# Attention and two MLPs in one kernel: the first part's weight sums move into the last slots of layer 1, the last output group is summed bank by bank, and the unused general path's transfers change queue

## The chip, the cores and the metric

One core of one Trainium2 chip runs the whole program. The metric is the device time of one execution in microseconds. TensorE is called PE here as in the profile, VectorE DVE, ScalarE ACT, GpSimd POOL and SyncE SP.

## The reference, cut to what matters

Attention with sinks and a window gives 1536 tokens of width 512. Two MLPs with 2048 inner columns follow; the second is the one that the change touches.

```
def _moe_ref(x, w_in, w_out, a, b):            # layer 1
    h = x @ w_in
    P = a[0] + a[1] * h + a[2] * h**2 + a[3] * h**3
    Q = 1.0 + abs(b[0]) * abs(h) + abs(b[1]) * h**2
    return (P / (Q + 1e-06)) @ w_out

def _moe2_ref(x, w_in, w_out):                 # layer 2
    h = np.maximum(x @ w_in, 0.0)
    return (h * h @ w_out)
```

The weights arrive as 64-bit floats and are converted on the chip. Every product is made of three matmuls on a high and a low part of each factor (high times high, high times low, low times high).

## The kernel before

**Slots of layer 1.** After the attention, the program is an order written out by hand. A step of layer 1 is one of 3 chunks of 512 tokens and one of 16 blocks of 128 inner columns, so there are 48 steps. In each slot PE gets twelve matmuls that make `h` of one step (`g1`, in `whole`, L635) and twelve that multiply the finished activation of an earlier step with the second weight (`g2`, L702). ACT, DVE and POOL work out the rational function between the two. The last of it is `act_c`: ACT writes the high part `gh` (L681) and POOL subtracts it from `g`, which gives the low part `gl` (L682). `gh` and `gl` have two buffers each. POOL also multiplies in L652, subtracts the high part of a converted weight in L282 (`w_fin`) and the high part of layer 1's output in L750 (`split_late`).

**Turns of layer 2.** Layer 2 works on four parts of four blocks each. The chunk of tokens 0 is multiplied in the plain way (`whole`). For chunks 1 and 2 a Winograd scheme takes seven products in place of eight for each of two pairs of blocks. It needs sums of the first weights (`weights_sums`: L794 and L801 on POOL, then a split into high and low, L805 on ACT and L806 on POOL) and sums of the tokens (`tokens_sums`: L815 on DVE, split by `tokens_split` through the same L805 and L806). `turn(n)` orders this by tables: `hs` says which products stand in a turn, `gs` in which turn which activation meets the second weight through `g2`, `ms` and `ss` where weight sums are made and split. The sums of the first part stand in turns 1 and 2 and their splits in turns 2 and 7. Turn 3 is the first with a `g2` of layer 2. Below, block 0 to block 3 are the four blocks of part 0 in chunk 0, whose `g2` stand in turns 3 to 6.

**Weights.** `jobs` is the list of loads and conversions. The first `LATE = 32 + AHEAD` weight tiles are converted during layer 1, the others in the turns that `CONV` names. All weights are also loaded a second time for a check of their size (L229 on DVE).

**The end.** The last four `g2`, those of part 3 and chunk 2, come one block after another, each over four PSUM banks. Then DVE adds each bank to the earlier partial sum (L736, in `finish`) and SP issues a transfer of 256 KB for each (L739). `verdict` reduces the checks to one flag, which all engines load (L1252). If it is not zero, `general()` computes everything again in a slower way; on these inputs it is zero, and each engine branches over that code (L1254) to the wait for all transfers and the end.

Of the kernel before, what the change touches and what calls it, by code (L numbers as in the profile page):

```python
# [15 lines left out]
P = 128  # L16
# [15 lines left out]
AHEAD = 10  # L32
# [3 lines left out]
CONV = (1, 9, 10, 12, 13, 15, 16, 17, 18, 19, 20, 22, 23, 27, 28, 29, 30, 31, 32, 34, 35, 36)  # L36
# [8 lines left out]
def kernel(  # L45
# [594 lines left out]
    def layers(mp, due):  # L640
# [44 lines left out]
        def g2(k):  # L685
            L, g, c, f = steps[k] if k in range(KL) else (1,) + k
            f0, f1 = part(L, g)[0], part(L, g)[1] - 1
            if f == f0:
                if f1 == NF - 1 and (L, c) == (1, NCH - 1):
                    acc[L, g, c] = [ps_t("T"), ps_t("T"), ps_t("U"), ps_s()[:, 0]]  # L690
                else:
                    acc[L, g, c] = [t[:, m] for t in [ps_s(), ps_s()] for m in range(2)]
# [89 lines left out]
        def setup_two():  # L782
            two["sum"], = tags(1)
            two["s"] = [tags(2), tags(2)]
            two["g"] = [t[:, j].bitcast(F32) for t in map(fresh, tags(4)) for j in range(2)]

        def weights_sums(p, r):
# [3 lines left out]
            y = z.rearrange("p a (b n) -> p (a b) n", b=2)  # L791
            for e in range(2):
                w = W[1, f + e, 0]
                nc.gpsimd.tensor_tensor(out=x[:, e], in0=w[0].bitcast(F32), in1=w[1].bitcast(F32), op=ALU.add)  # L794
            hw = DM // 2
            a11, a12, a21, a22 = (x[:, e, j * hw:(j + 1) * hw] for e in range(2) for j in range(2))
            for dst, i0, i1, op in (
                (y[:, 0], a21, a22, ALU.add), (y[:, 1], y[:, 0], a11, ALU.subtract),
                (y[:, 2], a11, a21, ALU.subtract), (y[:, 3], a12, y[:, 1], ALU.subtract),
            ):  # L800
                nc.gpsimd.tensor_tensor(out=dst, in0=i0, in1=i1, op=op)  # L801
            two["S", r] = lambda: split(z, fresh(tag[0]), fresh(tag[1]))
# [87 lines left out]

        def turn(n):
# [12 lines left out]
            if n == 3:  # L904
                tokens_sums()
            if n in hs:
# [7 lines left out]
            if n + 1 in gs:  # L914
                key = gs[n + 1]
                g = gq.pop(("f", key))
                act_c(key, g)
                two["g"].append(g)
            if n in ss:
                r = "S", ss[n]  # L920
                two[r] = two[r]()
            for j in ((2,), (3,), (1,), (4, 0))[n - 3] if 3 <= n < 7 else ():
                tokens_split(j)
            if n in ms:
                weights_sums(*ms[n])
# [3 lines left out]
        def slot(k, mid=None, after=None):  # L929
# [16 lines left out]
            split_late()  # L946
            w_until(due(k))
            if 0 <= k - 2 < K:
                g2(k - 2)
            if k + 1 - K in gs:  # L950
                g2(gs[k + 1 - K])
            if after:
                after()
            if k + 1 - K == ends2:
                finish(0)
                finish(1)

        return slot, K + ends2


# [40 lines left out]
    def general():  # L1001
        with ExitStack() as gx:
# [16 lines left out]
            with tc.tile_pool(name="ga", bufs=1) as ga:  # L1019
# [7 lines left out]
                for b in range(B):  # L1027
                    nc.sync.dma_start(out=kt, in_=k[b].rearrange("(r e) d t -> (e d) r t", e=2))
                    for i in range(NB):
                        nc.sync.dma_start(  # L1030
                            out=vt[:, i], in_=v[b, :, i * P:(i + 1) * P, :].rearrange("h p d -> p h d")
                        )
                    for i in range(NB):
                        nc.sync.dma_start(
# [66 lines left out]
            with tc.tile_pool(name="gm", bufs=1) as gm:  # L1101
                for L in range(2):
                    wg = [gm.tile([P, NF, DM], F32, name=f"wg{j}") for j in range(2)]
                    for f in range(NF):
                        for j in range(2):
                            src = ((w_in1, w_out1), (w_in2, w_out2))[L][j].bitcast(I32)
                            r = gs.tile([P, DM, 2], I32, tag="gr", name="gr")
                            if j == 0:
                                nc.sync.dma_start(
# [3 lines left out]
                            else:  # L1113
                                nc.sync.dma_start(
# [24 lines left out]
                    for c in range(NCH):  # L1139
# [59 lines left out]
                        for m in range(4):  # L1199
# [3 lines left out]
                            else:  # L1203
# [3 lines left out]
                                nc.sync.dma_start(out=out[r0:r0 + P, :], in_=o)  # L1207
# [20 lines left out]
    slot, slots = layers(mp, due)  # L1228
# [25 lines left out]
    with tc.If(flag != 0):  # L1254
# [40 lines left out]
```

## Time and profile before

| what | value |
|---|---|
| median of 3 runs | 604.63 us (604.2 to 605.49) |
| the profiled execution, its own time | 605.5 us |
| its span | 603.7 us |
| granted clock of PE, mean | 0.994 |
| busy in the span | PE 588.8, DVE 441.3, POOL 414.6, ACT 386.0 us |

The span is from the first to the last instruction, and 1.8 us of the execution's own time lie around it. A matmul that is listed with 0.39 us overlaps the next one; twelve of them back to back take 2.72 us.

### The profile page before, as it was taken

Reading aid. Unit: us, or ns where it says so; the run is one execution under the profiler, and the core shown is the slowest. Engines: PE = TensorE matmul, PEld = TensorE weight load, DVE = VectorE, ACT = ScalarE, POOL = GpSimd, SP = SyncE. Lnnn points to the kernel's source line nnn. Section 1 sums busy time; section 2 is a strip of 40 time slices with the busy share of each in tenths; the row PEclk is TensorE's granted clock in tenths of the full one; section 3 lists DMA queues with packets and bytes.
Section 4 is the critical chain, followed back from the end, with each engine's and each line's share of the span. In section 5 each row is a group of like instructions: output and inputs, shape, how many; then the busy total and the mean of one; then the engine's idle time right before and its main releaser. Section 6 shows DMA issues by size and latency. Waiting matters only on the chain.

```text
span 603.7 us, 9762 instructions
## 1 busy us (share of the span) xinstructions
PE 588.8 (98%) x3442; PEld 483.5 (80%) x3442; DVE 441.3 (73%) x875; ACT 386.0 (64%) x792; POOL 414.6 (69%) x373
## 2 busy tenths in 40 slices
PE   8999999999999999999999989999999999999995
PEld 6787788788888878888888868888888888888884
DVE  5989759998989989768767583887774886524452
ACT  5989768788886877877869545454634453444330
POOL 4799878677776766766858899287935594566231
PEclk9999999999999999999999999999999999999998
DMA  8976313333333232211111415556634645633022
GB/s 209 301 209 179 89 38 105 105 104 97 86 99 80 95 104 71 69 36 35 36 35 36 141 34 175 175 176 216 200 113 169 208 143 171 211 104 104 26 109 81
DMA packets 64232, 72.05 MB, mean 119 GB/s; under 512 B 15280, under 2 KB 55216, under 8 KB 64176
## 3 DMA queue, kind: packets, MB, share of 16 engines
q1 hardware_dynamic: 64032, 71.35, 38.1%
q8 instruction: 29, 0.48, 0.3%
q14 instruction: 27, 0.22, 0.1%
q10 hardware_dynamic: 144, 0.00, 0.0%
HBM read 68.20 MB, written 3.15 MB: 118 GB/s over the span
## 4 chain that ended last, share of the span: by engine, by line
PE 69%; DVE 17%; ACT 8%; issue 2%; POOL 2%; DMA 1%; DVEq 0%; ACTq 0%
PE s L702 31%; PE T L635 16%; PE T L852 9%; PE U L852 4%; DVE t L674 3%; PE O L477 2%; DVE U L672 2%; ACT gh L681 2%; DVE ns L394 2%; ACT U L666 2%; ACT U L667 2%; ACT w L281 2%; DVE s L384 2%; DVE t L670 2%; PE U L635 1%
## 5 line engine op out<-in xcount | busy, mean ns | idle before, releaser
L635 PE MATMUL T<-xh,w 128*128 128x512 f32 x480 | 158.4, 391 | 0.4 <-DVE t L656 0.4
L702 PE MATMUL s<-gh,w 128*128 128x512 f32 x384 | 126.1, 389 | 0.0
L682 POOL TENSOR_TENSOR gl<-two,gh 128x512 fp32r<-128x512 f32 x48 | 62.2, 1298 | 73.0 <-ACT gh L681 69.8
L702 PE MATMUL s<-w,gh 128*128 128x512 f32 x360 | 111.9, 392 | 0.0
L635 PEld LDWEIGHTS T<-xh,w 128*128 128x128 f32 x480 | 90.1, 188 | 21.5 <-DVE t L656 2.3
L635 PE MATMUL T<-xl,w 128*128 128x512 f32 x240 | 93.5, 389 | 0.0
L282 POOL TENSOR_TENSOR w<-wx,w 128x512 fp32r<-128x512 f32 x64 | 83.0, 1298 | 14.0 <-ACT w L281 13.4
L682 POOL TENSOR_TENSOR gl<-t,gh 128x512 fp32r<-128x512 f32 x48 | 62.2, 1296 | 39.8 <-ACT gh L681 38.9
L652 POOL TENSOR_TENSOR t<-t,ah 128x512 f32<-128x512 f32 x48 | 62.3, 1298 | 34.4 <-ACT t L649 32.5
L702 PEld LDWEIGHTS s<-gh,w 128*128 128x128 f32 x384 | 72.1, 188 | 14.9
L702 PEld LDWEIGHTS s<-w,gh 128*128 128x128 f32 x360 | 68.4, 190 | 14.3
L702 PE MATMUL s<-gl,w 128*128 128x512 f32 x192 | 74.7, 389 | 0.0
L702 PE MATMUL s<-w,gl 128*128 128x512 f32 x180 | 70.9, 394 | 2.3 <-POOL gl L682 2.3
L681 ACT CAST gh<-two 128x512 fp32r<-128x512 f32 x48 | 29.5, 618 | 45.9 <-PE s L702 45.8
L681 ACT CAST gh<-t 128x512 fp32r<-128x512 f32 x48 | 29.8, 622 | 44.8 <-DVE t L674 39.2
L670 DVE SCALAR_TENSOR_TENSOR t<-t,U 128x512 f32<-128x512 f32 x48 | 32.9, 686 | 28.9 <-ACT U L667 28.8
L635 PEld LDWEIGHTS T<-xl,w 128*128 128x128 f32 x240 | 45.1, 188 | 9.0
L281 ACT CAST w<-wx 128x512 fp32r<-128x512 f32 x57 | 35.1, 618 | 21.5 <-PE s L702 10.9
L413 ACT ACTIVATE pe<-ns,nmax 128x136 f32<-128x136 f32 (+1 forms) x96 | 38.0, 400 | 6.7 <-DVE nmax L394 6.6
L702 PEld LDWEIGHTS s<-gl,w 128*128 128x128 f32 x192 | 36.0, 188 | 7.6
L702 PEld LDWEIGHTS s<-w,gl 128*128 128x128 f32 x180 | 34.1, 189 | 9.8 <-POOL gl L682 2.7
L736 DVE TENSOR_TENSOR part<-s,part 128x512 f32<-128x512 f32 x33 | 21.3, 686 | 27.4 <-PE s L702 26.8
(184 smaller groups left out, 1249.0 us busy)
## 6 DMA issues: line engine op xcount, KB each, us to landing
wr<-in_w_in_dram SPq DMA_DIRECT2D x54, 512.0 KB, 3.8
wr<-in_w_out_dram SPq DMA_DIRECT2D x52, 512.0 KB, 3.9
qr<-in_q_dram SPq DMA_DIRECT2D x12, 256.0 KB, 5.6
keys<-in_k_dram SPq DMA_DIRECT2D x12, 256.0 KB, 5.2
vr<-in_v_dram SPq DMA_DIRECT2D x12, 256.0 KB, 5.6
wr<-in_v_dram SPq DMA_DIRECT2D x6, 512.0 KB, 3.9
out_dram<-part SPq DMA_DIRECT2D x12, 256.0 KB, 2.0
vsc<-in_v_dram SPq DMA_DIRECT2D x2, 16.0 KB
```

The costliest lines, as they stand in the source:

```text
L281: (nc.gpsimd.tensor_copy if conv["tag"] == "U" else nc.scalar.copy)(out=t[:, 0], in_=xf)
L282: nc.gpsimd.tensor_tensor(out=t[:, 1], in0=xf, in1=t[:, 0].bitcast(F32), op=ALU.subtract)
L413: nc.scalar.activation(out=t[:, e, 0:w], in_=ns[e][:, 0:w], func=ACTF.Exp, scale=-1.0, bias=nmax[:, ix:ix + 1], accum_out=rs[:, 2 * pr + e ...
L635: nc.tensor.matmul(h, lhsT=wi[a][:, kk * P:(kk + 1) * P], rhs=(xh, xl)[b][c][:, kk, :], start=(kk == 0 and a + b == 0), stop=(kk == KD - 1 ...
L652: nc.gpsimd.tensor_tensor(out=t, in0=t, in1=ah, op=ALU.mult)
L670: nc.vector.scalar_tensor_tensor(out=t, in0=t, scalar=QP, in1=r0, op0=ALU.add, op1=ALU.mult)
L674: nc.vector.scalar_tensor_tensor(out=t3, in0=t3, scalar=fa[:, 0:1], in1=r0, op0=ALU.add, op1=ALU.mult)
L681: nc.scalar.copy(out=gh, in_=g)
L682: nc.gpsimd.tensor_tensor(out=gl, in0=g, in1=gh.bitcast(F32), op=ALU.subtract)
L702: nc.tensor.matmul(acc[L, g, c][m], lhsT=lh, rhs=rh, start=(f == f0 and a + b == 0), stop=(f == f1 and a == 1),)
L736: nc.vector.tensor_tensor(out=q, in0=src, in1=q, op=ALU.add)
L852: nc.tensor.matmul(two[r][bank], lhsT=w[a][:, kk * P:(kk + 1) * P], rhs=x[b][:, kk, :], start=(j in (1, 5, 6, 7) and kk == 0 and a + b == ...
```

## The change

It has four pieces. The first part's weight sums are made by a generator that is stepped once in each of the last slots of layer 1, from 14 slots ahead of turn 0 on (`BEFORE`), and the buffers for them are taken there. To free these buffers two fewer weight tiles are converted in layer 1 (`AHEAD`), and `CONV` gets two entries more. In a turn, `act_c` now stands ahead of the products, and block 2's activation is split into a buffer of its own in turn 3 (`whole_g`). The last output group leaves the turns: its four activations are split ahead into buffers of their own, and `last_group` runs all twelve matmuls of one bank, has it added and sent, and goes to the next bank. The flag is loaded after the first of these banks. In `general`, all transfers are issued by ACT in place of SP.

```
-AHEAD = 10
+AHEAD = 8
+BEFORE = 14
-CONV = (1, 9, 10, 12, 13, ...
+CONV = (2, 5, 6, 9, 10, 12, 13, ...
...
+        def last_group(between):
+            c = NCH - 1
+            finish(0)
+            finish(1)
+            for m, d in enumerate([ps_t("T"), ps_t("T"), ps_t("U"), ps_s()[:, 0]]):
+                for f in tail:
+                    gg, wo = gq[LP, c, f], W[1, f, 1]
+                    for a, b in ((0, 0), (0, 1), (1, 0)):
+                        nc.tensor.matmul(
+                            d, lhsT=gg[a][:, m * P:(m + 1) * P], rhs=wo[b],
+                            start=(f == tail[0] and a + b == 0), stop=(f == tail[-1] and a == 1),
+                        )
+                q = parts[c, m // 2][0][:, m % 2].bitcast(F32)
+                nc.vector.tensor_tensor(out=q, in0=d, in1=q, op=ALU.add)
+                nc.sync.dma_start(out=out[c * CT + m * P:c * CT + (m + 1) * P, :], in_=q)
+                if m == 0:
+                    between()
...
-            for r, (a, b) in enumerate(((1, 2), (5, 6) if p else (2, 7))):
-                ms[h0 + a], ss[h0 + b] = (p, r), r
-        ends2 = max(gs)
+            for r, a in enumerate((1, 5)):
+                if p:
+                    ms[h0 + a], ss[h0 + a + 1] = (p, r), r
+        LP, ends2 = len(CUTS[1]) - 2, max(gs) - 3
+        tail = [4 * LP + i for i in (0, 1, 3, 2)]
+        for i in range(4):
+            del gs[ends2 + i]
+        h0 = ends2 - 10
+        whole_g = {h0 + r: (LP, 2, f) for r, f in zip((5, 4, 7, 9), tail)}
+        whole_g[3] = (0, 0, 2)
...
+            pool = nc.gpsimd.tensor_tensor
             for e in range(2):
                 w = W[1, f + e, 0]
...
+                pool(out=x[:, e], in0=w[0].bitcast(F32), in1=w[1].bitcast(F32), op=ALU.add)
+                yield
+            pool(out=y[:, 0], in0=a21, in1=a22, op=ALU.add)
+            pool(out=y[:, 1], in0=y[:, 0], in1=a11, op=ALU.subtract)
+            yield
+            pool(out=y[:, 2], in0=a11, in1=a21, op=ALU.subtract)
+            pool(out=y[:, 3], in0=a12, in1=y[:, 1], op=ALU.subtract)
+            yield
+            hi, lo = two["S", r] = fresh(tag[0]), fresh(tag[1])
+            nc.scalar.copy(out=hi, in_=z)
+            for j in range(2):
+                pool(out=lo[:, j], in0=z[:, j], in1=hi[:, j].bitcast(F32), op=ALU.subtract)
+                yield
...
+        def sums_turn(n):
+            if n == -BEFORE:
+                setup_sums()
+                first.extend(weights_sums(0, r) for r in range(2))
+            if n < 1:
+                while first and next(first[0], 1):
+                    first.pop(0)
+            if n in ms:
+                first.append(weights_sums(*ms[n]))
+            if n in ms or n in ss:
+                for _ in range(4 if n in ms else 3):
+                    next(first[0], None)
+            if n in ss:
+                first.pop(0)
...
+            if n + 1 in gs and gs[n + 1] not in gq:
+                key = gs[n + 1]
+                g = gq.pop(("f", key))
+                act_c(key, g)
+                two["g"].append(g)
+            if n in whole_g:
+                key = whole_g[n]
+                g = gq.pop(("f", key))
+                tag, = tags(1)
+                t = fresh(tag)
+                extra[key] = tag
+                gq[key] = split(g, t[:, 0], t[:, 1])
+                two["g"].append(g)
             if n in hs:
...
             split_late()
+            sums_turn(k + 1 - K)
             w_until(due(k))
...
-                    nc.sync.dma_start(out=kt, in_=k[b].rearrange("(r e) d t -> (e d) r t", e=2))
+                    nc.scalar.dma_start(out=kt, in_=k[b].rearrange("(r e) d t -> (e d) r t", e=2))
...
-        if n == slots - 6:
+        if n == slots - 3:
             last = verdict()
             next(last)
-        if n == slots - 3:
-            fl = next(last)
-        if n == slots - 2:
-            flag = nc.values_load(fl, min_val=0, max_val=12 * P)
+    fl = next(last)
+    flag = []
+    last_group(lambda: flag.append(nc.values_load(fl, min_val=0, max_val=12 * P)))
```

POOL's order at the start of layer 2, before. L794 and L801 are the weight sums (`two<-w` and the four halves), L806 is a low part of a split, L682 is a `gl`:

```order
L682 TENSOR_TENSOR gl<-t_4018,gh 128x512
L282 TENSOR_TENSOR w<-wx,w 128x512
L794 TENSOR_TENSOR two<-w 128x512 x2
L801 TENSOR_TENSOR two<-two 128x256 x4
L682 TENSOR_TENSOR gl<-t_4068,gh 128x512
L282 TENSOR_TENSOR w<-wx,w 128x512
L682 TENSOR_TENSOR gl<-two,gh 128x512
L806 TENSOR_TENSOR two<-two 128x1024
L794 TENSOR_TENSOR two<-w 128x512 x2
L801 TENSOR_TENSOR two<-two 128x256 x4
L682 TENSOR_TENSOR gl<-two,gh 128x512
L806 TENSOR_TENSOR two<-two 128x1024
```

The same place in the change, where the lines have moved (L683 is `gl`, L283 the converted weight, L839 the low part of a split):

```order
L683 TENSOR_TENSOR gl<-t_4025,gh 128x512
L283 TENSOR_TENSOR w<-wx,w 128x512
L683 TENSOR_TENSOR gl<-t_4074,gh 128x512
L683 TENSOR_TENSOR gl<-two,gh 128x512
L283 TENSOR_TENSOR w<-wx,w 128x512
L683 TENSOR_TENSOR gl<-two,gh 128x512
L839 TENSOR_TENSOR two<-two 128x512
L839 TENSOR_TENSOR two<-two 128x1024
L839 TENSOR_TENSOR xl_84<-part,xh_81 128x1024
L683 TENSOR_TENSOR gl<-two,gh 128x512
```

The second `gl<-two` of each list is that of block 1. Ahead of it stood two sets of sums and a split, and now there stands none; the `two<-two 128x512` behind it is block 2's, in its own buffer.

POOL's order some ten slots earlier, in layer 1, in the change (L653 is the multiplication that was L652, L766 the low part of layer 1's output, L823 to L829 the sums, L834 the two halves of their low part):

```order
L825 TENSOR_TENSOR two<-two 128x256
L826 TENSOR_TENSOR two<-two 128x256
L683 TENSOR_TENSOR gl<-t_3424,gh 128x512
L653 TENSOR_TENSOR t<-t,ah 128x512
L766 TENSOR_TENSOR xl_82<-part,xh_79 128x512
L828 TENSOR_TENSOR two<-two 128x256
L829 TENSOR_TENSOR two<-two 128x256
L683 TENSOR_TENSOR gl<-t_3473,gh 128x512
L653 TENSOR_TENSOR t<-t,ah 128x512
L766 TENSOR_TENSOR xl_82<-part,xh_79 128x512
L834 TENSOR_TENSOR two<-two 128x512
L683 TENSOR_TENSOR gl<-t_3523,gh 128x512
```

Each slot has one step of the sums at its end, behind what POOL did there before.

SP's last rows, of before, up to the first of the 102 transfers that stand in the general path:

```order
L739 DMA out_dram<-part 128x512 x8
L1252 TENSOR_LOAD fl
L1252 ISA x2
L739 DMA out_dram<-part 128x512 x4
L1254 COMPARE_AND_BRANCH
L1028 DMA gkt<-in_k_dram 128x4x768
L1030 DMA gvt<-in_v_dram 128x8x64 x6
L1034 DMA gqt<-in_q_dram 128x4x128 x6
```

And of the change (L755 is the transfer in `finish`, L723 the one in `last_group`):

```order
L755 DMA out_dram<-part 128x512 x8
L723 DMA out_dram<-part 128x512
L1305 TENSOR_LOAD fl
L1305 ISA x2
L723 DMA out_dram<-part 128x512 x3
L1307 COMPARE_AND_BRANCH
L1307 UNCONDITIONAL_BRANCH x2
```

One transfer of the last group now stands ahead of the load of the flag, and SP's branch has no code left to jump over.

## Rows read from the trace of the kernel before

**Rows 1.** The page: busy time by engine.
```profile
PE 588.8 (98%) x3442; PEld 483.5 (80%) x3442; DVE 441.3 (73%) x875; ACT 386.0 (64%) x792; POOL 414.6 (69%) x373
```

**Rows 2.** What PE waited for: us in total, times, longest.
```profile
PE s L702 <- POOL gl L682: 2.3, 1, 2.3
...
PE s L370 <- DVE nmax L394: 1.3, 1, 1.3
```

**Rows 3.** The chain that ended last, 340 to 372 us: start, us.
```profile
347.04 2.35 POOL two L806
349.39 2.52 POOL two L794 x2
...
351.98 1.61 POOL two L801
...
358.62 1.25 POOL gl L682
...
359.91 6.92 PE s L702 x22
...
368.19 2.72 PE s L702 x12
```

**Rows 4.** PE's timeline at the wait: start, us, idle before.
```profile
357.04 0.61 PE L702 MATMUL s<-w,gh 128*128 128x512 f32 x2
359.91 0.50 PE L702 MATMUL s<-w,gl 128*128 128x512 f32 x1 [2.26 <-POOL gl L682]
...
366.66 1.52 PE L852 MATMUL T<-two 128*128 128x512 f32 x6
```

**Rows 5.** Busy time by stretch; PE first; third from the end the granted clock.
```profile
357.00:359.00 2.00, 0.65 (x3) 0.19 (x2) 2.00 (x3) 1.76 (x3) 2.00 (x2) 1.00 0.00 0
...
361.00:363.00 2.00, 2.00 (x7) 1.59 (x6) 0.59 (x1) 0.00 (x0) 2.00 (x2) 0.58 0.95 352
```

**Rows 6.** POOL's groups by form, 240 to 345 us: busy, mean ns, idle before.
```profile
L682 POOL TENSOR_TENSOR gl<-t,gh 128x512 fp32r<-128x512 f32 x20 | 25.9, 1293 | 13.2 <-ACT gh L681 13.2
L652 POOL TENSOR_TENSOR t<-t,ah 128x512 f32<-128x512 f32 x18 | 23.4, 1302 | 16.5 <-ACT t L649 16.5
...
L801 POOL TENSOR_TENSOR two<-two 128x256 f32<-128x256 f32 x4 | 2.9, 738 | 0.2
L794 POOL TENSOR_TENSOR two<-w 128x512 f32<-128x512 f32 x2 | 2.6, 1300 | 0.0
```

**Rows 7.** The same, 345 to 378 us.
```profile
L806 POOL TENSOR_TENSOR two<-two 128x1024 fp32r<-128x1024 f32 x3 | 7.2, 2395 | 0.0
L801 POOL TENSOR_TENSOR two<-two 128x256 f32<-128x256 f32 x4 | 6.6, 1661 | 0.2
```

**Rows 8.** DVE's timeline, first and last of four token sums.
```profile
351.76 1.22 DVE L815 TENSOR_TENSOR part<-part 128x1024 f32<-128x1024 f32 x1
...
356.27 1.76 DVE L815 TENSOR_TENSOR part<-part,two 128x1024 f32<-128x1024 f32 x1
```

**Rows 9.** ACT's timeline: block 1's high part, the first token sum's high part.
```profile
350.49 0.62 ACT L681 CAST gh<-two 128x512 fp32r<-128x512 f32 x1 [1.51 <-PE s L702]
354.70 1.06 ACT L805 CAST two<-two 128x1024 fp32r<-128x1024 f32 x1 [3.58 <-DVE two L815]
```

**Rows 10.** DVE's timeline at the end: the last addition.
```profile
597.21 0.69 DVE L736 TENSOR_TENSOR part<-s,part 128x512 f32<-128x512 f32 x1
```

**Rows 11.** Line L739, the output transfers: issue ns, first and last start; landing.
```profile
L739 SPq DMA_DIRECT2D out_dram<-part x12: 332/332/348, 571.7 to 597.9; - x12
...
DMA to landing us min/median/max: 2.0/2.0/4.2
```

**Rows 12.** SP's own waits, the one at the branch.
```profile
SPq L1254 <- SPq L1254: 3.6, 3, 2.8
```

**Rows 13.** Busy time by stretch at the end; last come DMA share and GB/s.
```profile
600.00:601.00 1.00, 0.00 (x0) 0.00 (x0) 0.00 (x0) 0.00 (x0) 0.00 (x0) 0.63 0.12 43
601.00:602.00 1.00, 0.00 (x0) 0.00 (x0) 0.00 (x0) 0.00 (x0) 0.00 (x0) 0.50 0.06 23
```

More of the change, by code (lines that the diff above doesn't have):

```diff
@@ L35 @@
 TURN = 12
-CONV = (1, 9, 10, 12, 13, 15, 16, 17, 18, 19, 20, 22, 23, 27, 28, 29, 30, 31, 32, 34, 35, 36)
+BEFORE = 14
+CONV = (2, 5, 6, 9, 10, 12, 13, 15, 16, 17, 18, 19, 20, 22, 23, 27, 28, 29, 30, 31, 32, 34, 35, 36)
 ORDER = (((0, 1), (0, 6)), ((0, 7), (0, 2)), ((0, 5), (0, 4)), ((1, 1), (0, 3)), ((1, 7), (1, 6)), ((1, 2), (1, 5)),
@@ L688, in g2 @@
             if f == f0:
[L689 to L692, printed above, removed]
+                acc[L, g, c] = [t[:, m] for t in [ps_s(), ps_s()] for m in range(2)]
             wo = W[L, f, 1]
@@ L768, in layers @@
                 gs[r] = (p, c, 4 * p + f)
[L769 to L771 removed]
+            for r, a in enumerate((1, 5)):
[8 more added lines that the diff above has]
+        whole_g[3] = (0, 0, 2)
+        extra = {}
         def fresh(tag):
@@ L780, in tags, with setup_sums, setup_two @@
             return [spare.pop(0) for _ in range(n)]
-        def setup_two():
+        def setup_sums():
             two["sum"], = tags(1)
             two["s"] = [tags(2), tags(2)]
+        def setup_two():
             two["g"] = [t[:, j].bitcast(F32) for t in map(fresh, tags(4)) for j in range(2)]
@@ L791, in weights_sums @@
             y = z.rearrange("p a (b n) -> p (a b) n", b=2)
+            hw = DM // 2
+            a11, a12, a21, a22 = (x[:, e, j * hw:(j + 1) * hw] for e in range(2) for j in range(2))
+            pool = nc.gpsimd.tensor_tensor
             for e in range(2):
                 w = W[1, f + e, 0]
[L794 to L802, printed above, removed]
+                pool(out=x[:, e], in0=w[0].bitcast(F32), in1=w[1].bitcast(F32), op=ALU.add)
[11 more added lines that the diff above has]
+                yield
         def split(src, hi, lo):
@@ L889, in after @@
                 summed((p, 2, f), "b", 6)
+        first = []
+        def sums_turn(n):
[12 more added lines that the diff above has]
+                first.pop(0)
         def turn(n):
@@ L913, in turn @@
                         product(p, r, j)
[L914 to L921, printed above, removed]
             for j in ((2,), (3,), (1,), (4, 0))[n - 3] if 3 <= n < 7 else ():
                 tokens_split(j)
-            if n in ms:
-                weights_sums(*ms[n])
         K = len(steps)
@@ L950, in slot @@
             if k + 1 - K in gs:
-                g2(gs[k + 1 - K])
+                key = gs[k + 1 - K]
+                g2(key)
+                if key in extra:
+                    spare.append(extra.pop(key))
             if after:
                 after()
[L954 to L958, printed above, removed]
+        return slot, K + ends2 - 1, last_group
     def verdict():
@@ L1033, in general @@
                     for i in range(NB):
-                        nc.sync.dma_start(
+                        nc.scalar.dma_start(
                             out=qt, in_=q[b, :, :, i * P:(i + 1) * P].rearrange("(r e) d t -> (e d) r t", e=2)
@@ L1108, in general @@
                             if j == 0:
-                                nc.sync.dma_start(
+                                nc.scalar.dma_start(
                                     out=r.rearrange("p (c f) t -> p c (f t)", c=KD),
@@ L1113, in general @@
                             else:
-                                nc.sync.dma_start(
+                                nc.scalar.dma_start(
                                     out=r.rearrange("p n t -> p (n t)"), in_=src[f * P:(f + 1) * P, :]
@@ L1206, in general @@
                                 r0 = c * CT + m * P
-                                nc.sync.dma_start(out=out[r0:r0 + P, :], in_=o)
+                                nc.scalar.dma_start(out=out[r0:r0 + P, :], in_=o)
     KB = 28
@@ L1226, in due @@
         return ends[stop[min(k + 1 - KL, len(stop) - 1)] - 1]
-    slot, slots = layers(mp, due)
+    slot, slots, last_group = layers(mp, due)
     with tc.tile_pool(name="ap", bufs=1) as ap:
@@ L1245 @@
         slot(n)
-        if n == slots - 6:
+        if n == slots - 3:
             last = verdict()
             next(last)
-        if n == slots - 3:
-            fl = next(last)
-        if n == slots - 2:
-            flag = nc.values_load(fl, min_val=0, max_val=12 * P)
+    fl = next(last)
+    flag = []
+    last_group(lambda: flag.append(nc.values_load(fl, min_val=0, max_val=12 * P)))
     main.close()
-    with tc.If(flag != 0):
+    with tc.If(flag[0] != 0):
         general()
```

2 lines of the change are left out of this document (1 added, 1 removed).

## The prediction

> **What bounds the kernel now.** The page comes first: PE is busy for 588.8 of 603.7 us, and no other engine for more than 441.3 [rows 1]. The change leaves every matmul of this path in the program, so it can win only from the 14.9 us in which PE stands still and from stretches where PE runs slowly. The waits of PE, read next, name one long one: 2.3 us, once, for a `gl` from POOL [rows 2]. The next longest is 1.3 us and lies in the attention, which is not touched. The chain that ended last shows where the 2.3 us come from: it leaves PE, runs through POOL from 347.04 us to 359.87 without returning (a split, two weight additions, the four halves, then `gl`), and enters PE again at 359.91 [rows 3]. PE's timeline shows the same place: two matmuls with the high part at 357.04, then nothing until the low part arrives [rows 4]. The stretches show what follows: before the wait the clock is granted in full, and from 361 to 363 us it is at 0.58 in the mean, which is time at the lower level (1.2 GHz) mixed with time at 2.4 [rows 5]. The last thing to see is the end of the span: DVE's last addition ends at 597.90 (597.21 + 0.69), and 5.8 us pass before the span ends [rows 10].
>
> **The sum at the start of layer 2.** From 357.04 to 366.66 PE does the 24 matmuls of blocks 1 and 2 and nothing else [rows 4]. At the usual pace twelve take 2.72 us [rows 3], so 24 take 5.44. The stretch took 9.62. The loss is 4.18 us: 2.3 of it is the wait, the other 1.9 the matmuls at the lower clock. The 1.3 us wait of the attention left no such trace, and this clock fell only after the 2.3 us wait, so I count both as one price, which goes if the wait goes.
>
> Does it go? Block 1's `gl` waits for two things, its high part and POOL's queue. The high part is written at 350.49 and done at 351.11 [rows 9], 7.5 us before POOL comes to `gl` at 358.62 [rows 3]. So the queue is the cause. The change takes out of that queue, between block 0's `gl` and block 1's, a split of 2.4 us, two additions (2.5) and the four halves (6.6) [rows 3, 7], and puts in one weight subtraction of 1.3. POOL is then free when the high part is done, at about 351.2, and needs 1.3 us [rows 6].
>
> What is late next? PE wants `gl` as the third matmul of each block. Without the wait block 1 is wanted at 357.5 (357.04 + 2 x 0.227), block 2 starts at 359.76 and wants its low part at 360.2, the first product with token sums starts at 362.5, and block 3's low part is wanted at 364.3. All of them pass through POOL while DVE makes the four token sums from 351.76 to 358.03 [rows 8]. There a half of the weight sums took POOL 1.661 us, and 0.738 in layer 1 [rows 6, 7]. So POOL and DVE hinder each other there. As a bound I let each POOL operation lose a whole DVE operation, 1.76 us [rows 8]. Block 1's is then done by 354.3 (351.2 + 1.76 + 1.3), block 2's by 357.3. The first token split starts behind it (its high part ends at 355.76 [rows 9]), waits for DVE until 358.0 and takes 2.4 [rows 7]: 360.4, ahead of 362.5. The second takes POOL to 362.8, and block 3's `gl` to 364.1, 0.2 us before it is wanted. With no hindrance the same list ends near 362. So no wait is left by the bound, but block 3 comes close, and DVE's list is longer too: behind the token sums it now has two conversions ahead of the first product's addition. Both ends: all 4.2 us gained, or a new wait of up to about 1.5 us at block 3 and the 1.9 us of clock again, which leaves 0.8. I take 4.2, since the bound itself still fits.
>
> The Trainium skill speaks to this place on its page SBUF — State Buffer, section Who interferes with whom: a DVE operation with two inputs in SBUF contends with a GpSimd operation that reads SBUF, and the second to start is blocked until the first has finished. The 1.661 against 0.738 us [rows 6, 7] agrees in direction. By that rule POOL's list is at its late bound, and the sum stays at 4.2 us with 0.2 to spare.
>
> **What the moved work costs in layer 1.** The sums and splits of both pairs are 2 x (2 x 1.30 + 4 x 0.738) and four halves of splits of 128x512 at about 1.3, together 16.3 us of POOL [rows 6]. Of these 5.5 stood in the stretch from 240 to 345 us already, so 10.8 are added, and two weight subtractions (2.6) leave it. Before, POOL idled there for 29.7 us (13.2 + 16.5) waiting for ACT [rows 6]. About 21 us of it remain, so the cover is wide on average. It is thin in single slots: `gl`, a weight, the multiplication, an output split and one step of the sums are 5 x 1.27 = 6.3 us in a slot of 24 matmuls, 5.44. By the order of the change one slot is that full, and the others hold four operations of 1.3 or three and a pair of halves, 5.0 to 5.2. An overrun of 0.9 us is made up in the next slots. ACT gets two casts of 1.06 us there [rows 9] and loses two weight casts. I cost all this at nothing; without cover it would be the 0.9 us of that slot.
>
> **The end.** PE's and DVE's last work is the same length in both orders: the last bank is complete with the last matmul, and its addition takes 0.69. What changes is how many transfers are under way. Before, four of 256 KB are issued within 2 us, the last at 597.9, and the slowest landing is 4.2 us, where the median is 2.0 [rows 11]. 597.9 + 4.2 = 602.1, and 1.6 us of closing waits follow. After it, the first three go out 2.72 us apart and the last is alone: if it lands like the median, the gain is 2.2 us. From 600 to 602 us only 43 and 23 GB/s still move, at a DMA share of 0.12 and 0.06 [rows 13]: one or two of the 16 engines are behind. If what holds them is not the queue of four, the gain is smaller, down to none. SP also has a wait of its own at the branch, 2.8 us [rows 12]. It starts when the last issue ends (598.3) and ends at 601.1, ahead of the landing at 602.1. If it stayed, the landing would no longer decide, and the gain would stop at 1.0. In the change SP has no code between the branch and its target. I take 1.8, nearer to the full 2.2 than to 1.0, because a backlog on one or two engines shrinks with three earlier transfers gone, though whatever delays them may still touch the last one.
>
> On SP's wait the Trainium skill, page Runtime: NRT & Kernel Launch, section Instruction fetch mechanics, says that a taken branch to code outside the fetched window costs a fetch of the target before execution goes on. By it SP's 2.8 us go with the general path's transfers, and the end gains up to 2.2 us; no run here shows SP's branch with little code behind it.
>
> **Edits at nothing.** ACT's transfers in the general path never run: the flag is zero. The flag is loaded behind the first bank with 36 matmuls still queued behind it, 8.2 us of cover. The activations of the last group are split ahead by POOL, which has two operations of 1.3 in a turn of 2.72 there. The two conversions moved to turns 2 and 5 are in the list above.
>
> **Rivals.** (a) Both gains as summed. (b) The wait moves to block 3 or to the first products of layer 2: for it speaks the 0.2 us of the late bound, against it that POOL and DVE took turns for one part of that time only. A wait of 0.5 us costs 0.5; one like the old one (1.5 and the clock) leaves 0.8 of the 4.2: 599.1 to 602.0. (c) The end gains 1.0 or nothing, by SP's wait or by engines that are behind for another reason: 599.4 to 600.4. (d) Slower: if the sums make POOL late in every one of the 12 slots by the 0.9 us of the fullest one, PE waits 10.8 us in layer 1, and the time is 598.6 + 10.8 = 609.4. It decides from 0.6 us a slot on (7.2 over 12, where the 6.0 are eaten and 0.2% more). Against it stand the 21 us of idle time. (e) The change does not do what it says: `gl` of block 1 stays where it was, because something else in POOL's queue waits as long. Then the end alone is left: 602.8. The free 7.5 us behind the high part speak against it.
>
> **The numbers.** 603.7 - 4.2 - 1.8 = 597.7 for the span; 1.8 us lie around it, so 599.5 for the profiled execution, which stands 0.87 above the median of 604.63: 598.6. Chances: (a) 0.65, with a range of its own from 597.9 to 599.6; (b) 0.15; (c) 0.13; (d) 0.04; (e) 0.03. The range from 597.7 to 601.0 holds (a), (c) and about half of (b). A measurement of this kernel tells 0.2%, 1.2 us, from no change; (a), (b) and (c) are faster by more, (e) mostly too, so faster gets 0.93, no change 0.03, slower 0.04.
>
> **What will show it.** Right: no wait of PE for `gl` over 0.5 us after 340 us, the granted clock in full through 370, product and `g2` of turns 4 to 9 back to back, POOL idle for some us between 340 and 350; in layer 1 POOL's idle time near 20 us; the last landing near 2 us, SP's branch wait gone. Wrong: a PE wait at a `gl` or at a token sum between 359 and 375, a low clock behind it, a landing of 4 us, or waits of PE for `h`'s bank (L635) before 345.

## The result, and the profile after

| | before | after |
|---|---|---|
| median, runs on the same chip | 605.49 us (604.2 to 606.1, 6 runs) | 599.73 us (599.26 to 601.07, 6 runs) |
| profiled execution, its own time | 605.5 us | 599.75 us |
| its span | 603.7 us | 597.9 us |
| granted clock of PE, mean | 0.994 | 1.0 |

The ratio is 0.9911, with a 95% interval from 0.9897 to 0.9925: faster by 0.9%, and the whole interval is more than 0.2% away from no change. The span shrinks by 5.8 us where 6.0 were forecast. The median lies 1.1 us above the forecast of 598.6 and inside its range. One effect is on no list so far: only tiles that are converted in layer 1 are loaded a second time, so with `AHEAD` two loads of 512 KB drop out (106 become 104).

The page's busy times, then what PE waited for (us in total, times, longest), answer to [rows 1] and [rows 2].

```profile
PE 587.1 (98%) x3442; PEld 482.6 (81%) x3442; DVE 440.4 (74%) x875; ACT 386.0 (65%) x792; POOL 413.5 (69%) x381
```
```profile
PE O L478 <- DVE xf L503: 1.9, 6, 0.7
PE s L371 <- DVE nmax L395: 1.3, 1, 1.3
```

The `gl` of the low part has left the list; the longest single wait is now the attention's 1.3 us. PE has the same 3442 matmuls in 1.7 us less busy time (588.8 - 587.1); they run faster in one stretch.

PE's timeline (start, us) at the place of [rows 4]. L700 is `g2`, L885 a product with token sums.

```profile
357.28 0.61 PE L700 MATMUL s<-w,gh 128*128 128x512 f32 x2
357.73 0.39 PE L700 MATMUL s<-w,gl 128*128 128x512 f32 x1
...
360.00 2.88 PE L700 MATMUL s<-w,two 128*128 128x512 f32 x12
362.72 1.52 PE L885 MATMUL T<-two 128*128 128x512 f32 x6
364.08 0.61 PE L700 MATMUL s<-w,gh 128*128 128x512 f32 x2
364.53 0.39 PE L700 MATMUL s<-w,gl 128*128 128x512 f32 x1
```

No row carries an idle time in brackets. Blocks 1 and 2 take 5.44 us (357.28 to 362.72) where they took 9.62. The stretches that answer to [rows 5] show PE busy throughout and the clock (third from the end) in full:

```profile
357.00:359.00 2.00, 2.00 (x10) 1.65 (x10) 2.00 (x4) 1.97 (x5) 1.78 (x1) 1.00 0.00 0
...
361.00:363.00 2.00, 2.00 (x11) 1.65 (x10) 1.90 (x4) 0.93 (x3) 2.00 (x2) 1.00 1.01 331
```

POOL's timeline over the same place answers to the chain of [rows 3]. L683 is a `gl`, L283 a converted weight, L839 the low part of a split; the bracket is the idle time ahead of the row.

```profile
345.99 1.29 POOL L683 TENSOR_TENSOR gl<-two,gh 128x512 fp32r<-128x512 f32 x1 [4.13 <-ACT gh L682]
347.24 1.28 POOL L283 TENSOR_TENSOR w<-wx,w 128x512 fp32r<-128x512 f32 x1
351.44 1.30 POOL L683 TENSOR_TENSOR gl<-two,gh 128x512 fp32r<-128x512 f32 x1 [2.91 <-ACT gh L682]
352.69 2.28 POOL L839 TENSOR_TENSOR two<-two 128x512 fp32r<-128x512 f32 x1
357.22 3.38 POOL L839 TENSOR_TENSOR two<-two 128x1024 fp32r<-128x1024 f32 x1 [2.25 <-ACT two L838]
360.57 2.42 POOL L839 TENSOR_TENSOR xl<-part,xh 128x1024 fp32r<-128x1024 f32 x1
362.96 1.29 POOL L683 TENSOR_TENSOR gl<-two,gh 128x512 fp32r<-128x512 f32 x1
364.21 2.41 POOL L839 TENSOR_TENSOR two<-part,two 128x1024 fp32r<-128x1024 f32 x1
```

POOL now waits for the high part, not the high part for POOL: block 1's `gl` starts at 351.44 in place of 358.62. It was wanted at 357.73, so 5 us are to spare. At block 3 they are few: the `gl` ends at 364.25 (362.96 + 1.29), and PE wants it at 364.53.

In layer 1 (240 to 345 us) POOL's groups, as in [rows 6], have more work and less idle time:

```profile
L683 POOL TENSOR_TENSOR gl<-t,gh 128x512 fp32r<-128x512 f32 x20 | 25.9, 1294 | 8.9 <-ACT gh L682 8.9
L653 POOL TENSOR_TENSOR t<-t,ah 128x512 f32<-128x512 f32 x18 | 23.4, 1300 | 11.2 <-ACT t L650 11.2
...
L834 POOL TENSOR_TENSOR two<-two 128x512 fp32r<-128x512 f32 x4 | 5.2, 1294 | 0.0
L823 POOL TENSOR_TENSOR two<-w 128x512 f32<-128x512 f32 x4 | 5.2, 1290 | 0.0
```

The idle time went from 29.7 to 20.1 us (8.9 + 11.2), and PE is busy for all of the 105 us, before and after.

The end: DVE's last addition, the landings of the last group's four transfers, SP's waits, and the stretches with DMA share and GB/s last; they answer to [rows 10 to 13].

```profile
593.28 0.69 DVE L722 TENSOR_TENSOR part<-s,part 128x512 f32<-128x512 f32 x1 [2.03 <-PE s L717]
```
```profile
DMA to landing us min/median/max: 2.0/2.0/3.2
```
```profile
SPq L1307 <- SPq L1307: 1.7, 2, 1.5
```
```profile
595.00:596.00 1.00, 0.00 (x0) 0.00 (x0) 0.00 (x0) 0.00 (x0) 0.00 (x0) 1.00 0.53 203
596.00:597.00 1.00, 0.00 (x0) 0.00 (x0) 0.00 (x0) 0.00 (x0) 0.00 (x0) 1.00 0.03 8
```

The addition starts 3.93 us earlier than in [rows 10]. From its end the program takes 3.9 us more (597.9 - 593.97) where it took 5.8. The data are through within the second microsecond; before, two slices with a share of 0.12 and 0.06 trailed behind them.

SP's longest wait needs care: the line L1307 holds the branch and, behind it, eight waits for transfers. Here are the start times of both (the branch is COMPARE_BRANCH, the waits are EVENT_SEMAPHORE, x8 their count), before and then after; the last row is the same view from 595 us on.

```profile
L1254 SPq EVENT_SEMAPHORE  x8: 17/17/17, 601.1 to 602.3; - x8
L1254 SPq COMPARE_BRANCH  x1: 45/45/45, 598.3 to 598.3; - x1
```
```profile
L1307 SPq EVENT_SEMAPHORE  x8: 17/17/17, 594.6 to 596.5; - x8
L1307 SPq COMPARE_BRANCH  x1: 50/50/50, 594.4 to 594.4; - x1
L1307 SPq EVENT_SEMAPHORE  x7: 17/17/17, 596.1 to 596.5; - x7
```

Before, SP needs 2.8 us from the branch to the next instruction, and in the change 0.2. The 1.5 us stand between the first and the second of the eight waits, from 594.6 to 596.1: there SP waits for the last transfer, which was issued at 594.0 and lands 2.1 us later. So the branch wait is gone, and the landing decides the end.

### The profile page after: what moved, and what is told of

Read it like the earlier page. It is cut to its first block, busy times and chain, and to the rows that moved or that the text cites. A ratio compares the mean times of both kernels' runs of the same rounds, so it can differ in the third digit from the quotient of the medians.

```text
span 597.9 us, 9759 instructions
## 1 busy us (share of the span) xinstructions
PE 587.1 (98%) x3442; PEld 482.6 (81%) x3442; DVE 440.4 (74%) x875; ACT 386.0 (65%) x792; POOL 413.5 (69%) x381
## 4 chain that ended last, share of the span: by engine, by line
PE 72%; DVE 17%; ACT 8%; issue 2%; DMA 0%; DVEq 0%; ACTq 0%
PE s L700 31%; PE T L636 17%; PE T L885 9%; PE U L885 4%; DVE t L675 3%; PE O L478 2%; DVE U L673 2%; DVE ns L395 2%; ACT U L667 2%; ACT U L668 2%; ACT gh L682 2%; PE U L636 2%; ACT w L282 2%; DVE s L385 2%; DVE t L671 2%
## 5 line engine op out<-in xcount | busy, mean ns | idle before, releaser
L700 PE MATMUL s<-gh,w 128*128 128x512 f32 x384 | 126.0, 389 | 0.0
L700 PE MATMUL s<-w,gh 128*128 128x512 f32 x344 | 105.9, 389 | 0.0
L683 POOL TENSOR_TENSOR gl<-two,gh 128x512 fp32r<-128x512 f32 x43 | 55.7, 1297 | 66.8 <-ACT gh L682 66.7
L283 POOL TENSOR_TENSOR w<-wx,w 128x512 fp32r<-128x512 f32 x64 | 83.0, 1298 | 15.2 <-ACT w L282 14.6
L683 POOL TENSOR_TENSOR gl<-t,gh 128x512 fp32r<-128x512 f32 x48 | 62.3, 1297 | 34.9 <-ACT gh L682 34.1
L700 PEld LDWEIGHTS s<-gh,w 128*128 128x128 f32 x384 | 72.1, 188 | 14.9
L653 POOL TENSOR_TENSOR t<-t,ah 128x512 f32<-128x512 f32 x48 | 62.2, 1297 | 29.1 <-ACT t L650 27.2
L700 PEld LDWEIGHTS s<-w,gh 128*128 128x128 f32 x344 | 64.6, 188 | 13.5
L700 PE MATMUL s<-gl,w 128*128 128x512 f32 x192 | 74.7, 389 | 0.0
L700 PE MATMUL s<-w,gl 128*128 128x512 f32 x172 | 66.9, 389 | 0.0
L682 ACT CAST gh<-t 128x512 fp32r<-128x512 f32 x48 | 29.9, 622 | 42.3 <-DVE t L675 38.9
L682 ACT CAST gh<-two 128x512 fp32r<-128x512 f32 x43 | 26.3, 617 | 36.7 <-PE s L700 36.6
L700 PEld LDWEIGHTS s<-gl,w 128*128 128x128 f32 x192 | 36.0, 188 | 7.6
L261 DVE SCALAR_TENSOR_TENSOR wx<-wr,O 128x512 int32<-128x512 int32 x57 | 39.0, 685 | 3.2
L230 DVE TENSOR_REDUCE wmin<-wr 128x1 f32<-128x512 f32 x64 | 41.1, 678 | 0.0
```

The lines of the kernel that those rows point to most:

```text
L230: nc.vector.tensor_reduce(out=dst, in_=src, axis=AX.X, op=op, apply_absolute_value=True)
L261: nc.vector.scalar_tensor_tensor(out=y, in0=low, scalar=29, in1=x, op0=ALU.logical_shift_right, op1=ALU.bitwise_or)
L283: nc.gpsimd.tensor_tensor(out=t[:, 1], in0=xf, in1=t[:, 0].bitcast(F32), op=ALU.subtract)
L653: nc.gpsimd.tensor_tensor(out=t, in0=t, in1=ah, op=ALU.mult)
L682: nc.scalar.copy(out=gh, in_=g)
L683: nc.gpsimd.tensor_tensor(out=gl, in0=g, in1=gh.bitcast(F32), op=ALU.subtract)
```

## The experiments

Ratios are to the kernel before on the same chip, with 95% intervals. To compare PE between profiles I take two matmuls by their number among the 3442: one of a step of `h` into bank `U` that starts at 345.25 before and 345.49 after, and the last one. Where a profile is 0.24 us late at the first and 3.93 early at the last, PE gained 4.17 us between the two. "Closing time" is from the last addition's start to the end of the span: 6.5 us before (603.7 - 597.21), 4.6 after.

**1. The sums alone.** The change with the old end and with the general path's transfers on SP. Block 2's buffer and the new order in a turn are still in it.

```
-        LP, ends2 = len(CUTS[1]) - 2, max(gs) - 3
...
-        whole_g = {h0 + r: (LP, 2, f) for r, f in zip((5, 4, 7, 9), tail)}
-        whole_g[3] = (0, 0, 2)
+        ends2 = max(gs)
+        whole_g = {3: (0, 0, 2)}
...
```

> The moved sums, the buffer of block 2 and the new order in a turn, with the end and the general path's queue as before. My theory: the wait of 2.3 us at block 1's low part goes and the lower clock behind it too, so 4.2 us less than before, a ratio of 0.993; from PE's last matmul to the end of the span 6.5 us as before. Rival (the lower clock comes from something else than the wait, or the sums cost something in layer 1): 2.3 us less or under, a ratio of 0.996 or more.

Measured: 601.54 us against 605.72, 0.9933 [0.9921, 0.9946]; span 599.7. No wait for `gl`, the clock at 1.0, and PE gains 4.17 us, as in the whole change. The end is that of before: closing time 6.6 us, SP's wait at its branch 3.0, the slowest landing 4.1.

```profile
SPq L1291 <- SPq L1291: 3.6, 2, 3.0
```

The first term of the sum is this piece, and no other piece is needed for it.

**2. The end bank by bank alone.** The kernel before with `last_group`, its four splits ahead, and the flag's new place.

```
+        for i in range(4):
+            del gs[ends2 + i]
...
+        whole_g = {h0 + r: (LP, 2, f) for r, f in zip((5, 4, 7, 9), tail)}
...
+    last_group(lambda: flag.append(nc.values_load(fl, min_val=0, max_val=12 * P)))
```

> The last group bank by bank alone, weight sums and general path's queue as before. My theory: the last landing comes down from about 4.2 to 2 to 3 us after its issue, but SP's wait of 2.8 us at its branch stays and now ends last, so the end gains 1.0 us, not 1.9; 0.998. Rival (SP's wait hides behind the landing whatever it is): 1.9 us, as in the whole change.

Measured: 605.06 against 605.72, 0.9993 [0.9983, 1.0003]: not to be told from no change. Closing time 5.8 us, 0.7 less, where 1.0 was expected. SP's wait stands in full:

```profile
SPq L1276 <- SPq L1276: 2.8, 1, 2.8
```

It starts at about 599.1 (the last issue begins at 598.8 and takes 0.34) and ends at 601.9, with the span's end 2.0 behind it. So the landing no longer decides, and SP does. The whole time has a loss in it, too: PE has a short stop at 581 us that neither before nor the change has: a third matmul starts 0.75 us after the first one, where 0.45 is usual, and the next after 0.34, where 0.23 is usual. That is 0.4 us together.

```profile
580.75 0.61 PE L699 MATMUL s<-w,gh 128*128 128x512 f32 x2
581.50 0.50 PE L699 MATMUL s<-w,gl 128*128 128x512 f32 x1
```

**3. The queue alone.** In the kernel before, `general` issues by ACT; one of the lines that change:

```
-                    nc.sync.dma_start(out=kt, in_=k[b].rearrange("(r e) d t -> (e d) r t", e=2))
+                    nc.scalar.dma_start(out=kt, in_=k[b].rearrange("(r e) d t -> (e d) r t", e=2))
```

> The general path's transfers on ScalarE's queue alone, all else as before. My theory: SP's wait of 2.8 us at its branch goes, but the last transfer still lands about 4.1 us after its issue and decides, so no change, within 0.2 us in the profile's end. Rival (the branch decides the end, or code fetched for it delays the transfers): the end shortens by 1 us or more.

Measured: 605.68 against 605.72, 1.0003 [0.9991, 1.0014]: the time does not move. SP's longest wait is 2.1 us in place of 2.8, but it is another one:

```profile
SPq L1254 <- SPq L1254: 3.1, 4, 2.1
```
```profile
L1254 SPq EVENT_SEMAPHORE  x8: 17/17/17, 598.6 to 601.7; - x8
L1254 SPq COMPARE_BRANCH  x1: 50/50/50, 598.4 to 598.4; - x1
```

From the branch to the next instruction SP needs 0.2 us; the 2.1 is a wait for a landing. It passes the wait for the last transfer, issued at 598.0, only at 601.5, and the span ends 1.6 later. So the theory holds: the branch wait goes, the landing decides. The landing took 3.5 us here, not 4.1, and the closing time is 5.8.

**4. The end and the queue together**, sums as before.

> Bank by bank and the general path's transfers on ScalarE's queue, weight sums as before. My theory: the end from the last matmul to the end of the span is 4.7 us as in the whole change, 1.9 less than before, 0.997; the wait at block 1 and the lower clock stay. Rival: the two edits add up from 1.0 and 0.

Measured: 603.99 against 605.72, 0.9978 [0.9969, 0.9987], a gain of 1.7 us where the two alone gave 0.7 and 0.0. Closing time 4.5 us. SP is through its branch in 0.2 us (598.1 to 598.3) and then waits 1.4 for the last transfer, which lands 2.1 us after its issue. PE has the stop of 0.4 us of run 2 here too. But PE's waits in this profile were a surprise:

```profile
PE s L699 <- POOL gl L682: 2.8, 2, 2.3
```

The 2.3 us wait is there, the clock stays at 1.00 behind it, and a second wait of 0.58 us follows. Runs 9 to 12 take this up.

**5. Without block 2's own buffer.**

```
-        whole_g[3] = (0, 0, 2)
```

> The whole change without the buffer of its own for block 2's split, which goes through the two common ones again. My theory: block 2's high part then waits for the second weight of block 0 to be multiplied (about 355.9 us), POOL takes it up two or three us later than now, still ahead of its use at 360.5; no wait of PE, or under 0.5 us, same time as the change. Rival (the list of POOL between 352 and 364 us has no room): a wait of PE of 1 us or more at block 2 or 3, and perhaps the lower clock behind it.

Measured: 600.15 against 605.44, 0.991 [0.9891, 0.9928], the same ratio as the change. One wait comes back at block 2:

```profile
PE s L700 <- POOL gl L683: 0.3, 1, 0.3
```

PE gains 3.58 us between the reference matmuls in place of 4.17. So the buffer is worth 0.6 us in the profile, less than the whole times can tell.

**6. The sums twice.** In the change, every addition, half and split of the moved sums is made twice in layer 1.

```
...
+                for _ in range(times):
+                    pool(out=x[:, e], in0=w[0].bitcast(F32), in1=w[1].bitcast(F32), op=ALU.add)
...
```

> The whole change with every POOL operation of the moved sums done twice in layer 1's last slots, 16.3 us of POOL work more in 12 slots; the result is unchanged. My theory: POOL has about 21 us idle from 240 to 345 us, but in the 12 slots it now has about 80 us of work for 71, so it falls behind by up to 9 us, of which the lead of its low parts over their use (4 to 5 us) hides half: PE waits 3 to 5 us in layer 1 and the time is 3 to 6 us longer than the change. Rival (the idle time spread over the stretch is cover enough): no wait, same time as the change.

Measured: 605.66 against 605.44, 1.0006 [0.9993, 1.0019]: the whole gain is gone. PE waits five times, all in layer 1. PE's waits, then POOL's groups, 240 to 345 us, with what is left of the idle time:

```profile
PE s L700 <- POOL gl L683: 4.3, 5, 1.7
```
```profile
L683 POOL TENSOR_TENSOR gl<-t,gh 128x512 fp32r<-128x512 f32 x19 | 24.6, 1295 | 3.4 <-ACT gh L682 3.4
L653 POOL TENSOR_TENSOR t<-t,ah 128x512 f32<-128x512 f32 x18 | 23.4, 1297 | 5.3 <-ACT t L650 5.3
```

8.7 us of POOL's idle time remain (3.4 + 5.3), and PE waits 4.3 us for `gl` all the same; at the first reference matmul it is 5.8 us later than in the change (6.05 - 0.24). The idle time of the whole stretch is not the cover of each slot in it.

**7 and 8. Block 1's `gl` late by five and by seven operations.** In the change, POOL repeats operations of 1.3 us ahead of that `gl`; the edit with five, where the second kernel has 7 for the 5:

```
...
+                if key == (0, 0, 1):
+                    z, hi, lo = two["again"]
+                    for j in range(5):
+                        nc.gpsimd.tensor_tensor(
+                            out=lo[:, j % 2], in0=z[:, j % 2], in1=hi[:, j % 2].bitcast(F32), op=ALU.subtract
+                        )
```

> The whole change with five POOL operations of 128x512 repeated ahead of block 1's low part, which brings the old wait back in a smaller form; the result is unchanged. By the timeline POOL is free at 348.5 us, and with what the token sums on VectorE do to it the five take until 357 to 358, so the low part comes at about 359 and PE waits about 1 us. My theory on the clock: a wait of about 1 us, like the 1.3 us in the attention, is followed by no lower clock, so the time grows by the wait alone, about 1 us. Rival: any wait of this kind costs the clock too, so 2.5 us or more.

> The same with seven operations: block 1's low part comes at about 362 us and PE waits about 4 us. My theory: the wait is followed by 3.4 us or so at the lower clock as before the change, so the time grows by the wait and 1.7 to 1.9 us more. Rival (the lower clock before the change had another cause, such as the burst of loads at 361 us): it grows by the wait alone.

Measured with five: 602.64 against 605.44, 0.9958 [0.9943, 0.9973]; with seven: 606.12, 1.0017 [1.0004, 1.003]. PE's rows with a wait, of the first and of the second kernel, and the stretch behind the wait of the second:

```profile
358.90 0.50 PE L700 MATMUL s<-w,gl 128*128 128x512 f32 x1 [1.11 <-POOL gl L683]
367.12 0.50 PE L700 MATMUL s<-w,gl 128*128 128x512 f32 x1 [1.13 <-POOL gl L683]
```
```profile
362.41 0.80 PE L700 MATMUL s<-w,gl 128*128 128x512 f32 x1 [4.56 <-POOL gl L683]
```
```profile
363.00:365.00 2.00, 2.00 (x6) 1.61 (x5) 1.90 (x5) 1.07 (x2) 2.00 (x2) 0.50 0.99 358
```

Five operations give two waits, at blocks 1 and 3, a full clock throughout, and PE loses 2.8 us of its 4.17. About 1 us was expected: the theory on the clock held, but the second wait was not foreseen. That the rival's 2.5 us or more came out is chance, since the clock it counted on stayed full. Seven give one wait of 4.56 us, 1.2 GHz behind it, and PE loses 6.2: the wait and 1.6 more, where 1.7 to 1.9 more was expected. The burst of loads is not what lowers the clock: it is there at the full clock too (331 GB/s in the change). The mechanism that the change removes can be put back by POOL's queue alone, and the lateness at block 1 travels on to block 3.

**9 to 12. The kernel before and the fourth kernel, two more profiles each.** Experiment 4 had thrown doubt on the lower clock as a part of the price.

> The kernel before, unchanged, profiled once more: is the lower clock behind the 2.3 us wait a matter of the program or of the single execution? Theory A (the execution): the 2.3 us wait is there in each profile, the 3.41 us at the lower clock (0.50) in some only, and a profile without them has a span about 1.7 us shorter, with a second short wait at block 3. Theory B (the program): here the lower clock follows again, for 3.4 us, span 603.0 to 604.0.

> The fourth experiment (end and queue changed together, sums as before), profiled again. Theory A (the execution): its lower clock may appear this time behind the 2.3 us wait; over the four profiles of this call both cases are seen, or at least one profile differs from the first one of its kernel. Theory B (the program): full clock again, with a second wait of about 0.6 us at block 3, span near 601.5.

> As the first of this call, one more profile: theory B wants the lower clock for 3.4 us in this one too; theory A leaves it open for each profile.

> As the second of this call, one more profile: theory B wants the full clock and the second wait in this one too; theory A leaves it open for each profile.

Measured, one time each: 605.1, 604.25, 605.14 and 603.78 us. The first of the two profiles of before has the full clock, the second the lower one. Their stretches, the clock third from the end:

```profile
361.00:363.00 2.00, 2.00 (x9) 1.66 (x10) 1.60 (x3) 0.00 (x0) 2.00 (x1) 1.00 0.87 233
363.00:365.00 2.00, 1.43 (x7) 0.88 (x6) 0.00 (x0) 1.35 (x2) 2.00 (x3) 1.00 1.07 358
```
```profile
361.00:363.00 2.00, 2.00 (x7) 1.52 (x6) 0.48 (x1) 0.00 (x0) 2.00 (x2) 0.50 0.97 371
363.00:365.00 2.00, 2.00 (x8) 1.57 (x7) 0.00 (x0) 1.47 (x2) 2.00 (x2) 0.68 1.00 279
```

And PE's waits in the first of them:

```profile
360.92 0.50 PE L702 MATMUL s<-w,gl 128*128 128x512 f32 x1 [2.25 <-POOL gl L682]
364.51 0.50 PE L702 MATMUL s<-w,gl 128*128 128x512 f32 x1 [0.57 <-POOL gl L682]
```

Both profiles of the fourth kernel had 1.2 GHz this time. So it belongs to the single execution, not to the program (theory A): of eight profiles with the 2.3 us wait, of four kernels, six have the lower clock and two do not. At the full clock PE comes sooner to the next low part, and waits 0.57 us for it. It is block 2's, the third matmul behind the rest of block 1, and not block 3's, as the expectation had it: POOL's list has a split of 2.4 us between the two `gl` [rows 3, 7]. Between the two reference matmuls this profile of before is 0.76 us faster than the first one (1.01 late at the first, 0.25 late at the last), not 1.7 as theory A had it; the fourth kernel's at the full clock is as much ahead of its other two, 0.7.

## Why the prediction was right, step by step

**The start of layer 2, 4.2 us.** PE gained 4.17 us between the reference matmuls, in the whole change and with the sums alone. That the queue and not the high part held block 1's `gl` is shown by runs 1 and 7: without the sums in the queue the wait is gone, with five operations put in it is back. Run 1 also has the new order in a turn, which was not tried by itself.

One step of the working was mis-sized: the 1.9 us "for the matmuls at the lower clock" were counted as the clock's price. At the full clock the same program still loses 3.4 us (4.17 - 0.76), since POOL is late for block 2 as well. The clock adds 0.76 us net; while PE runs slowly, POOL catches up. The other runs of before fit, as far as a mean over the span can tell: those with a mean granted clock of 0.998 or more have a median 1.2 us (chip of runs 1 to 4, 7 of 29 runs) and 0.7 us (chip of runs 5 to 8, 11 of 26) below those with 0.996 or less. Most of the 1.9 is thus the queue's price too, which goes in either case, and the total came out as forecast.

**What is late next.** Block 3 was to be done 0.2 us ahead of PE by the late bound; the profile has 0.28 (364.53 - 364.25). The parts differ from the bound's: the first split started at 357.22, not 358.0, but took 3.38 us beside DVE's last token sum, where the others take 2.4, and block 2's took 2.28 in place of 1.29. That the sums of these parts agree is in part luck. Rival (b) came this close. Run 7 is the rival as a kernel: 2.8 us of the gain eaten by waits at blocks 1 and 3.

By the rule of the Trainium skill (SBUF — State Buffer, Who interferes with whom) the prediction put POOL's list at its late bound, 364.1, and the list ended at 364.25. The rule itself fits the single operations: the second to start lost about what was left of the first (last section). The bound took a whole operation of 1.76 us for each loss, and there each was about 1.0.

**Layer 1 at nothing.** The idle time fell to 20.1 us (about 21 forecast), and no wait arose. Rival (d), POOL late in layer 1, did not come. But the 21 us held against it were the wrong measure: run 6 shows that PE waits while 8.7 us are still idle. The decisive number is what the fullest slots can take: one helping of the sums fits, two do not.

**The end, 1.8 us.** The closing time went from 6.5 to 4.6, 1.9 us. Two more profiles of before have 5.9 (603.4 - 597.46) and 6.3 (603.4 - 597.08), so the change is worth 1.3 to 1.9 there. The forecast's account of it holds: the end comes 1.6 to 1.9 us after the later of two things, SP's way through its branch and the landing of the last transfer.

| runs | branch to next instruction | issue to landing of the last transfer | closing time |
|---|---|---|---|
| before, 1, 9, 11 | 2.8 to 3.0 us | 3.5 to 4.1 us | 5.9 to 6.6 us |
| 2 (end alone) | 2.8 | hidden behind the branch | 5.8 |
| 3 (queue alone) | 0.2 | 3.5 | 5.8 |
| after, 4, 10, 12 | 0.2 | 2.1 to 2.2 | 4.5 to 4.6 |

The landing is read here from the moment at which SP passes its wait for that transfer. Only both together give the full gain. If SP's wait stayed, the gain was to stop at 1.0; run 2 is that case and has 0.7, since SP still goes through its eight waits behind the branch (602.0 to 602.5). SP's wait went and the landing came near the median of 2.0, as the forecast had it. The 1.8 was a value between 1.0 and the full 2.2; the full 2.2 was missed by 0.2 us at the landing (4.1 to 2.1, not 4.2 to 2.0) and by closing waits of 1.8 us where 1.6 were taken. In run 9, with the old end, the landing took 3.5 us (598.2 to 601.7), so the old end itself varies, and with it the gain. The code has not vanished: it lies behind ACT's branch now, which ACT passes long before the end (583.1 to 585.5).

The Trainium skill's rule on a taken branch (Runtime: NRT & Kernel Launch, Instruction fetch mechanics) fits the rows: 2.8 to 3.0 us with 102 transfers behind SP's branch in five profiles, 0.2 us without them in five. That the time goes into a fetch is not shown by them.

**The median.** The profiled execution came out at 599.75 us against 599.5. Of the 1.1 us by which the median is above 598.6, 0.86 is the base: three runs of before had 604.63, and with three more beside the change the median of six is 605.49. So most of the 0.87 us should not have been taken off for the profiled execution. By the median alone, 599.73 lies 0.1 us above the range of (a) (597.9 to 599.6) and inside that of (c), a smaller gain at the end; it is the profile, with its 4.17 and 1.9 us, that decides for (a).

## What to carry to other kernels

A wait behind a queue is priced by following the late engine to its next deadlines: the 2.3 us wait was worth 3.4 to 4.2 us, because POOL was late for the next block too, or PE ran at 1.2 GHz meanwhile. Move work into an engine's idle time only as fast as its fullest slot allows; the sum of idle time said 20 us, and a second helping of 16 us already made PE wait 4.3. At a program's end, ask for everything that must be over before it: shortening the last landing or the last branch alone gave 0.7 and 0.0 us, both together 1.7.

## What the runs showed of the hardware

**The same wait, two clocks.** A wait of PE of 2.25 to 2.26 us was followed by 1.2 GHz in six profiles of eight and by 2.4 GHz in two; two programs showed it both ways. Waits of 1.1 and 1.7 us never brought it, one of 4.56 us did. What decides in a single execution is open.

**A stop costs more than its length.** Where the clock stayed full, PE lost 2.8 us by two waits of 2.24 together (run 7): some 0.3 us more for each stop. About half is the overlap of a matmul with the next, which a stop loses (0.39 listed, 0.227 apart); 0.11 more is the first matmul behind it, 0.50 in place of 0.39. By that estimate before loses 2.25 + 0.57 + 0.6 = 3.4 at the full clock, which is what it lost; run 6, with five stops, 4.3 + 1.5 = 5.8, and it lost 5.8.

**POOL beside DVE.** DVE's four token sums in the change:

```profile
352.01 1.81 DVE L848 TENSOR_TENSOR part<-part 128x1024 f32<-128x1024 f32 x1
353.85 2.19 DVE L848 TENSOR_TENSOR two<-part 128x1024 f32<-128x1024 f32 x1
355.97 1.21 DVE L848 TENSOR_TENSOR part<-part 128x1024 f32<-128x1024 f32 x1
357.11 1.21 DVE L848 TENSOR_TENSOR part<-part,two 128x1024 f32<-128x1024 f32 x1
```

The last two take 1.21 us; no POOL operation was running when they started. POOL's splits at 352.69 and 357.22 start while a sum has 1.1 us to go, and take 2.28 and 3.38 us where 1.29 and 2.40 are usual. The sum at 353.85 starts while POOL's split has 1.1 us to go, and takes 2.19. So the one that starts second loses about 1.0 us, the rest of the other's operation; the 1.76 us of [rows 8] was itself such a lengthened sum.

**A branch over unused code.** SP needed 2.8 to 3.0 us from its branch to the next instruction with 102 transfers of the general path in its queue, and 0.2 us without them.

**Four transfers in a row.** The last of four of 256 KB landed 3.5 to 4.1 us after its issue when they went out 0.7 us apart, and 2.1 to 2.2 when 2.7 apart. What holds it back is open.
